# Joining the linear-attention block and its output projection into one interleaved block, with dummy matmuls beside it

## The chip, the cores and the metric

The kernel runs on one core of a Trainium2 chip. The metric is device time in microseconds (us) of one execution; a run's number is a median over executions. Engines are named as the profile names them: PE is the matrix engine, PEld its weight loads, DVE the vector engine, ACT the scalar engine, POOL and SP the other two. "Granted clock" is the share of full speed that PE's throttle allowed.

## The reference, cut to what matters

```python
x = A_x                                     # 1 x 2048 x 512, bf16; 32 heads of 16
x = x + _A_ref(_layernorm(x), A_wqkv, A_wo) # linear attention
x = x + _B_ref(_layernorm(x), B_wqkv, B_wo) # sliding-window softmax attention
x = x + _A_ref(_layernorm(x), A_wqkv, A_wo)
x = x + _B_ref(_layernorm(x), B_wqkv, B_wo)
# _A_ref: pq, pk = phi(q), phi(k)
#   kv = einsum(pk, v);  z = sum of pk over the sequence
#   o  = (pq kv) / (pq z + 1e-6);  return o @ wo
```

Only the two linear layers (first and third) are touched. I call them layer 1 and layer 3.

## The kernel before

The sequence is 16 tiles of 128 tokens. A linear layer is three blocks, and every engine waits for every other at the end of each: qkv, attention, output projection. The last two, cut to what matters (T is 16, f runs over four groups of eight heads):

```python
def phase_attn_A(self, first):
    # PE
    for f in range(4):                       # KV sums over all tokens
        for t in range(T): pe.matmul(pkv[:, f, 0:129], self.pk[:, t, ...], self.vA[:, t, f, 0:129], ...)
    for t in range(T):                       # denominators, 8 columns a matmul, two slots
        if t >= 2: pe.wait_ge(s_dcp.h, s_dcp.v(t - 1))
        for f in range(4): mm = pe.matmul(pden[sl][:, f * 8 : (f + 1) * 8], self.pqT[:, f, ...], self.Zs[:, f, :], ...)
        s_den.inc(mm)
    for t in range(T):                       # numerators, two slots
        if t >= 2: pe.wait_ge(s_od.h, s_od.v(t - 1))
        for f in range(4): mm = pe.matmul(pnum[:, sl, ...], self.pqT[:, f, ...], self.KV8[:, f, :], ...)
        s_num.inc(mm)
    # DVE: ... KV8, Zs; den_all + 1e-6 for 16 tiles; then
    v.wait_ge(s_r.h, s_r.v(1))
    for t in range(T):
        v.wait_ge(s_num.h, s_num.v(t + 1))
        s_od.inc(v.tensor_tensor(self.o_tok[:, t, :]..., pnum[:, sl, :]..., self.den_all[:, t, :]..., ALU.mult))
    # ACT: one reciprocal for all tiles, as Exp(-Ln(x)); a table is loaded in between
    a.wait_ge(s_dcp.h, s_dcp.v(T)); a.activation(flat, flat, ACT.Ln, ...); a.drain()
    s_r.inc(a.activation(flat, flat, ACT.Exp, ..., scale=-1.0))

def phase_wo(self, w_o, last, first, from_tok):      # a new block
    # PE, per tile: transpose o_tok (4 x 128x128), ACT copies it to SBUF, then 4 matmuls 128x512
    emit_transposes(pe, 0)
    for t in range(T):
        if t + 1 < T: emit_transposes(pe, t + 1)
        emit_matmuls(pe, t)
    # DVE, per tile
        s_res.inc(v.tensor_tensor(self.xres[:, t, :], pwo[:, sl, :], self.xres[:, t, :], ALU.add))
        if not last and t >= 1:
            v.bn_stats(self.ln_stats[:, t - 1, :], self.xres[:, t - 1, :])   # for the next layer's norm
```

The softmax here doesn't subtract the row's maximum and nothing guards it: scores larger than these inputs give would overflow.

## Time and profile before

| | before |
|---|---|
| median of 6 runs (lowest to highest) | 850.41 us (849.14 to 852.0) |
| span of the profiled execution | 847.4 us |
| layer 1, first multiply to last statistic | 34.59 us |
| layer 3, the same | 35.55 us |
| denominators to first multiply, layers 1 / 3 | 7.30 / 7.23 us |

The page of the kernel before: busy time and share of each engine, and the granted clock in tenths over 40 equal slices of the span.

```profile
...
PE 674.5 (80%) x5796; PEld 335.7 (40%) x5824; DVE 597.8 (71%) x2784; ACT 614.1 (72%) x856; POOL 6.5 (1%) x24
...
PEclk9989577996555555555779995979955555555559
...
```

No engine is busy throughout, and the clock falls to 5 in slices where PE still does work. An average over the whole span doesn't say what bounds one stage, so the next views look at the two changed layers alone.

The timeline of DVE in layer 1, kernel before. The columns are start, duration of the merged group, engine, line of the kernel, operation, output and inputs with sizes, count, and in brackets the idle time before it and what ended it.

```profile
...
97.66 0.30 DVE L580 TENSOR_SCALAR den_all<-pden 128x32 f32<-128x32 f32 x2 [0.26 <-PE pden L535]
100.82 11.04 DVE L586 TENSOR_TENSOR o_tokA<-pnum,den_all 128x512 bf16<-128x512 f32 x16 [2.86 <-ACT den_all L600]
115.38 0.69 DVE L681 TENSOR_TENSOR xres<-pwo,xres 128x512 bf16<-128x512 f32 x1 [3.52 <-PE pwo L646]
116.86 0.69 DVE L681 TENSOR_TENSOR xres<-pwo,xres 128x512 bf16<-128x512 f32 x1 [0.79 <-PE pwo L646]
117.47 0.69 DVE L684 BATCH_NORM_STATS2 ln_stats<-xres 128x6 f32<-128x512 bf16 x1
118.07 0.68 DVE L681 TENSOR_TENSOR xres<-pwo,xres 128x512 bf16<-128x512 f32 x1
...
```

The 16 multiplies take 11.04 us, 0.69 us each. They are in pairs: a closer look shows one start 0.60 us after the last and the next 0.79 us after it, because with two slots the PE's numerators are in line every second time. Then DVE waits 3.52 us for the first projection: block change, transposes, ACT copy and matmuls in series. After a slow start it alternates adds and statistics at about 0.595 us from start to start. Here 48 DVE instructions at 0.6 us, 28.6 us of work, take 34.59 us.

Busy time by stage, kernel before, layer 1. The columns are the stretch, its length, then PE, PEld, DVE, ACT and POOL busy (with instruction counts), granted clock, DMA share and GB/s.

```profile
...
93.52:100.82 7.30, 3.80 (x72) 2.92 (x72) 2.36 (x17) 2.73 (x3) 0.00 (x0) 0.64 0.00 0
100.82:111.86 11.04, 8.45 (x56) 4.81 (x56) 10.32 (x16) 0.00 (x0) 0.00 (x0) 0.50 0.00 0
111.86:115.38 3.52, 2.54 (x14) 1.61 (x16) 0.00 (x0) 1.08 (x2) 0.00 (x0) 0.50 0.02 5
115.38:135.41 20.03, 16.40 (x114) 8.87 (x114) 19.24 (x32) 9.64 (x15) 0.00 (x0) 0.98 0.00 0
...
```

PE is at half clock through the multiplies and the gap, and reaches full clock only with the dense projection. Its timeline at that place, same kernel:

```profile
...
112.18 1.01 PE L631 MATMUL pstwo<-ident,o_tokA 128*128 128x128 bf16 x8 [1.05 <-PEq L511]
113.86 1.49 PE L646 MATMUL pwo<-wA_o,oTtA 128*128 128x512 bf16 x3 [0.66 <-ACT oTtA L671]
...
116.66 0.39 PE L631 MATMUL pstwo<-ident,o_tokA 128*128 128x128 bf16 x4
...
```

Eight transposes take 1.01 us here; four take 0.39 us later, when the clock is at 1.00.

### The profile page before, as it was taken

The numbers are of one execution on the slowest core, as the hardware profiler recorded it, in microseconds if no ns is written. First come the engines' busy times: TensorE is split into PE (matmuls) and PEld (weight loads), VectorE is DVE, ScalarE is ACT, GpSimd is POOL, SyncE is SP. The second block draws the span as 40 slices with busy tenths as digits, with TensorE's granted clock in tenths as the row PEclk, the third lists the DMA queues.
The fourth block names the chain that finished last, engine by engine and source line by source line (L and its number), as shares of the span: only waits on it lengthen the run. The fifth ranks groups of instructions, "written<-read, shape, count | busy, mean of one in ns | idle before, by whom it ended". The sixth has DMA issues, their size and how long they took to land. (4 is left out here: it accounts for less than half of the span.)

```text
span 847.4 us, 16703 instructions
## 1 busy us (share of the span) xinstructions
PE 674.5 (80%) x5796; PEld 335.7 (40%) x5824; DVE 597.8 (71%) x2784; ACT 614.1 (72%) x856; POOL 6.5 (1%) x24
## 2 busy tenths in 40 slices
PE   0778685997888888888858876878888888888878
PEld 0343553443343443434533344434334434344344
DVE  6669676336878878788767775934488787887765
ACT  1678135448999999999557751455599999999983
POOL 1000000000000000000000000000000000000000
PEclk9989577996555555555779995979955555555559
DMA  8000000000000000000000000000000000000002
GB/s 297 0 1 1 1 1 2 1 1 1 1 2 1 2 2 1 2 1 2 1 1 0 1 1 1 1 1 2 0 2 1 2 2 2 2 1 2 1 2 100
DMA packets 5972, 9.46 MB, mean 11 GB/s; under 512 B 384, under 2 KB 4992, under 8 KB 5888
## 3 DMA queue, kind: packets, MB, share of 16 engines
q1 hardware_dynamic: 5472, 6.29, 2.2%
q0 software_dynamic: 416, 2.10, 0.7%
q8 instruction: 47, 0.77, 0.4%
q14 instruction: 37, 0.30, 0.1%
HBM read 6.29 MB, written 2.10 MB: 10 GB/s over the span
## 5 line engine op out<-in xcount | busy, mean ns | idle before, releaser
L811 ACT ACTIVATE PTs<-st,zero 128x768 bf16<-128x768 f32 (+2 forms) x512 | 404.8, 860 | 21.2 <-PE st L766 9.3
L848 DVE TENSOR_TENSOR PTs<-PTs,maskHi 128x128 bf16<-128x128 bf16 x1024 | 219.6, 220 | 78.7 <-ACT PTs L811 78.1
L785 PE MATMUL U<-vB,PTs 128*128 128x17 bf16 x2880 | 163.2, 179 | 66.5 <-DVE PTs L852 61.7
L785 PEld LDWEIGHTS U<-vB,PTs 128*128 128x128 bf16 x2880 | 116.3, 106 | 243.5 <-DVE PTs L852 227.6
L852 DVE TENSOR_TENSOR PTs<-PTs,maskLo 128x128 bf16<-128x128 bf16 x896 | 195.1, 218 | 0.0
L766 PE MATMUL st<-qT,kT 16*128 16x384 bf16 (+2 forms) x512 | 121.6, 473 | 2.2 <-PEq L321 2.2
L766 PE MATMUL st<-qT,kTB 32*128 32x384 bf16 (+2 forms) x512 | 122.5, 474 | 0.0
L339 PE MATMUL pst<-ident,xn 128*128 128x128 bf16 x256 | 30.7, 277 | 71.6 <-DVE xn L437 66.8
L377 PE MATMUL pss<-xnT,wB_qk 128*128 128x512 bf16 x248 | 61.2, 387 | 0.8 <-issue 0.4
L377 PE MATMUL pss<-wA_qkv,xnT 128*128 128x512 bf16 x255 | 61.6, 384 | 0.1
L681 DVE TENSOR_TENSOR xres<-pwo,xres 128x512 bf16<-128x512 f32 x64 | 43.6, 681 | 24.4 <-PE pwo L646 24.4
L399 ACT ACTIVATE xnT<-pst 128x512 bf16<-128x512 bf16 x64 | 34.8, 595 | 31.8 <-PE pst L339 31.5
L471 DVE TENSOR_SCALAR kTB<-kT,maskB 128x512 bf16<-128x512 bf16 x32 | 11.3, 353 | 64.2 <-ACT kT L418 64.2
L252 ACT ACTIVATE tmpE<-pss,zero 128x512 f32<-128x512 f32 x64 | 44.1, 689 | 15.4 <-PE pss L377 8.5
L339 PEld LDWEIGHTS pst<-ident,xn 128*128 128x128 bf16 x256 | 20.4, 120 | 84.5 <-DVE xn L437 51.0
L671 ACT ACTIVATE oTtA<-pstwo 128x512 bf16<-128x512 bf16 x32 | 18.9, 597 | 42.0 <-PE pstwo L631 42.0
L828 DVE TENSOR_TENSOR o_tok<-U,densb 128x128 bf16<-128x128 f32 x128 | 37.3, 292 | 9.6
L253 ACT ACTIVATE tmpR<-pss,zero 128x512 bf16<-128x512 f32 x64 | 44.0, 687 | 0.0
L256 DVE TENSOR_SCALAR tmpE<-tmpE 128x512 f32<-128x512 f32 x64 | 26.9, 421 | 23.3 <-ACT tmpR L253 23.2
L418 ACT ACTIVATE qT<-pss 128x512 bf16<-128x512 f32 x32 | 19.1, 597 | 32.5 <-PE pss L377 32.5
L437 DVE TENSOR_SCALAR xn<-xres,ln_mv,ln_rstd 128x512 bf16<-128x512 bf16 x64 | 26.1, 431 | 18.2 <-PE pst L339 7.4
L377 PEld LDWEIGHTS pss<-wA_qkv,xnT 128*128 128x128 bf16 x256 | 25.6, 100 | 32.2 <-issue 3.6
(77 smaller groups left out, 639.8 us busy)
## 6 DMA issues: line engine op xcount, KB each, us to landing
xres<-in_A_x_dram SPq DMA_DIRECT2D x4, 512.0 KB, 5.4
out_dram<-xres SPq DMA_DIRECT2D x16, 128.0 KB, 1.7
wA_qkv<-in_A_wqkv_dram SPq DMA_DIRECT2D x1, 1536.0 KB, 10.2
wB_nat<-in_B_wqkv_dram POOLq DMA_DIRECT2D x1, 1536.0 KB, 9.1
wA_o<-in_A_wo_dram SPq DMA_DIRECT2D x1, 512.0 KB, 12.3
wB_o<-in_B_wo_dram POOLq DMA_DIRECT2D x1, 512.0 KB, 9.6
```

The source lines that it names most:

```text
L252: a.activation(self.tmpE[:, js, :], ps_ap, ACT.Exp, bias=z)
L253: return a.activation(self.tmpR[:, js, :], ps_ap, ACT.Relu, bias=z)
L339: mm = pe.transpose(pst[sl2][:, kt, :], self.xn[:, sl2, kt * P : (kt + 1) * P], self.ident[:])
L377: mm = pe.matmul(pss[:, sl, :], lhsT, rhs, start=(kt == 0), stop=(kt == 3))
L399: s_cp.inc(a.activation(self.xnT[:, :, t * P : (t + 1) * P], pst[sl2][:], ACT.Copy))
L681: s_res.inc(v.tensor_tensor(self.xres[:, t, :], pwo[:, sl, :], self.xres[:, t, :], ALU.add))
L766: mm = pe.matmul(ST[sl][:, e, 0:n], lhsT, rhs, start=True, stop=True, tile_position=(32 * (hs % 4), 0))
L785: mm = pe.matmul(ut[:, hs, 0:17], lhsT, rhs, start=(ci == 0), stop=(ci == len(cl) - 1))
L811: a.activation(self.PTs[:, j % NJS, hp[0] : hp[0] + 2, 0:n], ST[sl][:, :, 0:n], ACT.Exp, bias=self.zero1[:], scale=DH ** -0.5,)
L828: v.tensor_tensor(self.o_tok[:, jd, fd * P : (fd + 1) * P].rearrange("p (h d) -> p h d", d=DH), ut[:, :, 0:DH], dsb.to_broadcast([P, 8, DH ...
L848: op = v.tensor_tensor(self.PTs[:, js, hs, 0:P], self.PTs[:, js, hs, 0:P], self.maskHi[:], ALU.mult)
L852: op = v.tensor_tensor(self.PTs[:, js, hs, 2 * P : 3 * P], self.PTs[:, js, hs, 2 * P : 3 * P], self.maskLo[:], ALU.mult,)
```

## The change

Intent: let DVE go from multiplies to adds without a gap, hide ACT's transposed copies and the PE's work behind DVE, and keep the PE's clock up by dummy matmuls where it would idle. Its core, cuts marked:

```diff
-                        self.phase_attn_A(first=(li == 0))
-                        self.phase_wo(self.wA_o, last=last, first=(li == 0), from_tok=True)
+                        self.phase_attnwo_A(first=(li == 0), last=last)
 ...
+            def pe_warm(pe, n):
+                for _ in range(n):
+                    pe.matmul(pkw[:, 3, :], w_o[:, 0, 0:P], w_o[:, 0, :], start=True, stop=True)
 ... (KV sums as before, denominators now in spare columns of the same PSUM tensor)
                     s_den.inc(mm)
+                    if t % 2 == 1:
+                        pe_warm(pe, 1)
+                pe.wait_ge(s_dcp.h, s_dcp.v(T))
+                pe_num(pe, 0)
+                pe_num(pe, 1)
+                pe_warm(pe, 11)
+                for t in range(1, T + 2):
+                    if t <= T:
+                        pe_trans(pe, t - 1)
+                    if t + 1 < T:
+                        pe_num(pe, t + 1)
                     if t >= 2:
-                        pe.wait_ge(s_od.h, s_od.v(t - 1))
- ... (numerators for all tiles)
+                        pe_wo(pe, t - 2)
 ... DVE
+                LAGD = 3
+                for t in range(T + LAGD):
+                    if t < T:
+                        dve_mult(t)
+                    if t >= LAGD:
+                        dve_add(t - LAGD)     # and the statistics of tile t - 4
 ... ACT: the transposed copies follow the Ln and Exp in the same block
```

No DVE or ACT instruction goes away. PE gets 19 more matmuls per layer.

More of the change, by code (lines that the diff above doesn't have):

```diff
@@ L492, in phase_qkv, with phase_attnwo_A @@
         self.commit_all()
-    def phase_attn_A(self, first):
+    def phase_attnwo_A(self, first, last):
         nc = self.nc
@@ L505, in phase_attn_A @@
         s_pm = self.sem("permB")
+        s_w = self.sem("ld_wAo")
+        s_wo = self.sem("wo")
+        s_res = self.sem("res")
+        s_out = self.sem("out")
+        s_tp = self.sem("tpw")
+        s_cp = self.sem("cpw")
+        s_stat = self.sem("lnstat")
+        s_rstd = self.sem("lnrstd")
+        NSW = 4
+        w_o = self.wA_o
         with (
-            nc.psum_tensor(self.uname("pkv"), [P, 4, 512], dt.float32) as pkv,
+            nc.psum_tensor(self.uname("pkw"), [P, 4, 512], dt.float32) as pkw,
@@ L508, in phase_attn_A @@
             nc.psum_tensor(self.uname("pnum"), [P, 2, 512], dt.float32) as pnum,
-            nc.psum_tensor(self.uname("pden"), [P, H], dt.float32) as pden0,
-            nc.psum_tensor(self.uname("pden"), [P, H], dt.float32) as pden1,
+            nc.psum_tensor(self.uname("pstA"), [P, 4, P], dt.bfloat16) as pstA0,
+            nc.psum_tensor(self.uname("pstA"), [P, 4, P], dt.bfloat16) as pstA1,
             nc.Block() as blk,
         ):
-            pden = [pden0, pden1]
+            pst = [pstA0, pstA1]
@@ new lines, in dslot, with pe_num @@
+            def dslot(t):
+                return pkw[:, t % 2, 256 : 256 + H]
+            def pe_num(pe, t):
+                sl = t % 2
+                if t >= 2:
+                    pe.wait_ge(s_od.h, s_od.v(t - 1))
+                mm = None
+                for f in range(4):
+                    mm = pe.matmul(
+                        pnum[:, sl, f * P : (f + 1) * P],
+                        self.pqT[:, f, t * P : (t + 1) * P],
+                        self.KV8[:, f, :],
+                        start=True,
+                        stop=True,
+                    )
+                s_num.inc(mm)
@@ new lines, in pe_trans, with pe_wo @@
+            def pe_trans(pe, t):
+                sl2 = t % 2
+                pe.wait_ge(s_od.h, s_od.v(t + 1))
+                if t >= 2:
+                    pe.wait_ge(s_cp.h, s_cp.v(t - 1))
+                mm = None
+                for f in range(4):
+                    mm = pe.transpose(pst[sl2][:, f, :], self.o_tok[:, t, f * P : (f + 1) * P], self.ident[:])
+                s_tp.inc(mm)
+            def pe_wo(pe, t):
+                sl = t % NSW
+                if t >= NSW:
+                    pe.wait_ge(s_res.h, s_res.v(t - NSW + 1))
+                pe.wait_ge(s_cp.h, s_cp.v(t + 1))
+                mm = None
+                for f in range(4):
+                    mm = pe.matmul(pkw[:, sl, :], self.oTt[:, t % 2, f, :], w_o[:, f, :], start=(f == 0), stop=(f == 3))
+                s_wo.inc(mm)
@@ L515, in _ @@
+            def pe_warm(pe, n):
+                for _ in range(n):
+                    pe.matmul(pkw[:, 3, :], w_o[:, 0, 0:P], w_o[:, 0, :], start=True, stop=True)
             @blk.tensor
             def _(pe):
+                if first:
+                    pe.wait_ge(s_w.h, s_w.emitted)
                 for f in range(4):
@@ L520, in _ @@
                         mm = pe.matmul(
-                            pkv[:, f, 0:129],
+                            pkw[:, f, 0:129],
                             self.pk[:, t, f * P : (f + 1) * P],
@@ L529, in _ @@
                 for t in range(T):
-                    sl = t % 2
                     if t >= 2:
@@ L535, in _ @@
                         mm = pe.matmul(
-                            pden[sl][:, f * 8 : (f + 1) * 8],
+                            dslot(t)[:, f * 8 : (f + 1) * 8],
                             self.pqT[:, f, t * P : (t + 1) * P],
@@ L542, in _ @@
                     s_den.inc(mm)
-                for t in range(T):
-                    sl = t % 2
-                    if t >= 2:
-                        pe.wait_ge(s_od.h, s_od.v(t - 1))
-                    mm = None
-                    for f in range(4):
-                        mm = pe.matmul(
-                            pnum[:, sl, f * P : (f + 1) * P],
-                            self.pqT[:, f, t * P : (t + 1) * P],
-                            self.KV8[:, f, :],
-                            start=True,
-                            stop=True,
-                        )
-                    s_num.inc(mm)
+                    if t % 2 == 1:
[9 more added lines that the diff above has]
+                        pe_num(pe, t + 1)
+                    if t >= 2:
+                        pe_wo(pe, t - 2)
             @blk.vector
@@ L572, in _ @@
                     v.wait_ge(s_kv.h, s_kv.v(f + 1))
-                    v.tensor_tensor(self.KV8[:, f, :], pkv[:, f, 0:P], self.blockmask[:], ALU.mult)
-                    v.tensor_copy(self.zc[:, f : f + 1], pkv[:, f, P : P + 1])
+                    v.tensor_tensor(self.KV8[:, f, :], pkw[:, f, 0:P], self.blockmask[:], ALU.mult)
+                    v.tensor_copy(self.zc[:, f : f + 1], pkw[:, f, P : P + 1])
                     v.drain()
@@ L577, in _, with dve_mult @@
                 for t in range(T):
-                    sl = t % 2
                     v.wait_ge(s_den.h, s_den.v(t + 1))
-                    s_dcp.inc(v.tensor_scalar(self.den_all[:, t, :], pden[sl][:], 1e-6, None, op0=ALU.add))
+                    s_dcp.inc(v.tensor_scalar(self.den_all[:, t, :], dslot(t), 1e-6, None, op0=ALU.add))
                 v.wait_ge(s_r.h, s_r.v(1))
-                for t in range(T):
+                def dve_mult(t):
                     sl = t % 2
@@ L592, in _, with dve_add @@
                     )
+                def dve_add(t):
+                    sl = t % NSW
+                    v.wait_ge(s_wo.h, s_wo.v(t + 1))
+                    s_res.inc(v.tensor_tensor(self.xres[:, t, :], pkw[:, sl, :], self.xres[:, t, :], ALU.add))
+                    if not last and t >= 1:
+                        v.wait_ge(s_res.h, s_res.v(t))
+                        v.bn_stats(self.ln_stats[:, t - 1, :], self.xres[:, t - 1, :])
+                LAGD = 3
[4 more added lines that the diff above has]
+                        dve_add(t - LAGD)
+                if not last:
+                    v.wait_ge(s_res.h, s_res.v(T))
+                    v.bn_stats(self.ln_stats[:, T - 1, :], self.xres[:, T - 1, :])
+                    v.drain()
+                    for t in range(T):
+                        v.bn_aggr(self.ln_mv[:, t, :], self.ln_stats[:, t, :])
+                    v.drain()
+                    s_stat.inc(v.nop())
             @blk.scalar
@@ L600, in _ @@
                 s_r.inc(a.activation(flat, flat, ACT.Exp, bias=self.zero1[:], scale=-1.0))
+                for t in range(T):
+                    sl2 = t % 2
+                    a.wait_ge(s_tp.h, s_tp.v(t + 1))
+                    if t >= 2:
+                        a.wait_ge(s_wo.h, s_wo.v(t - 1))
+                    s_cp.inc(a.activation(self.oTt[:, sl2, :, :], pst[sl2][:], ACT.Copy))
+                if not last:
+                    a.wait_ge(s_stat.h, s_stat.v(1))
+                    s_rstd.inc(self._ln_rstd(a))
+            if last:
+                @blk.sync
+                def _(e):
+                    for t in range(T):
+                        e.wait_ge(s_res.h, s_res.v(t + 1))
+                        s_out.inc(e.dma_start(self.out[0, t * P : (t + 1) * P, :], self.xres[:, t, :]), 16)
+                    e.wait_ge(s_out.h, s_out.v16(T))
         self.commit_all()
```

## The prediction

> **What bounds the kernel now.** The change touches the linear-attention layers only (first and third of four). There the timeline shows three serial pieces. (a) KV sums and denominators, then ACT's Ln and Exp with a table load between: from 97.97 us (last denominator copy) to 100.8 PE and DVE have no useful work. (b) 16 DVE multiplies (o_tok), 11.04 us, while ACT idles for 12 us. They follow each other at 0.69 us, but in pairs 0.60 and 0.79: with two slots and the clock at 0.50, every second multiply waits for the PE. (c) A block change, transposes and first projection matmuls on a cold PE: DVE idles 3.5 us (4.2 in layer 3). Then DVE alternates 16 residual adds and 16 statistics at 0.595 us each, about 19.9 us. From first multiply to last statistic: 34.6 us (100.82 to 135.4) in layer 1, 35.5 us in layer 3. DVE work in it is 48 instructions x 0.6 = 28.6 us; the rest is pairing stalls and the gap. Nothing else of the 850 us is changed.
>
> **What the change does.** One block instead of two. DVE interleaves multiply(t), add(t-3), statistics(t-4); no DVE instruction is removed. PE interleaves transpose, numerator and projection. Removed: the 3.5 to 4.2 us gap and the pairing stalls (1.5 us). Added: 19 dummy 128x512 matmuls per layer, eight among the denominators, eleven in the Ln/Exp wait, to keep PE's clock up. The Trainium skill ("TensorE: Matmul & The Clock Gate", Part 1) says that idle PE drops to half clock and returns after about 3.4 us of sustained work; this trace agrees (0.50 all through (b), 1.00 about 2 us after dense projection in layer 1, 4.6 us in layer 3).
>
> **Cost.** Full-clock PE work per tile in the fused loop: transposes plus projection take 1.09 us per tile in the trace; numerators add some 0.22: 1.3 us against DVE's 1.79. So DVE sets the pace, and the loop takes 28.6 us plus 0.5 to 1 us of filling bubbles. Cold, PE work doubles to about 2.6 us per tile and PE would set the pace until the clock returns. PE would be some 72% busy when warm; the cold numerator stage streamed about 62% and never warmed up, so the hold is not certain. Dummies among denominators: that stage runs on a 0.54 us round trip per two tiles, half of it idle; a dummy costs 0.22 us warm (hidden) or 0.43 cold, so 0.2 to 1.2 us per layer. The eleven take 2.4 us warm, in a wait of about 2.9 us; 4.7 if cold, which delays the first transposes by about 1 us.
>
> All of this lies on the critical path, since the next layer's normalisation needs all statistics. Saved: layer 1 about 4.3 us, layer 3 about 5.3; less about 1 us for a clock that is cold part of the time.
>
> **Prediction.** 841.5 us, range 837 to 848. Faster by over 2%: 0.03; within 2%: 0.95; slower by over 2%: 0.02.
>
> **What would show it.** Timeline: first multiply to last statistic about 29.5 to 31 us in each of the two layers; DVE without idle in the loop's middle; ACT's transposed copies starting within 2 us of the first multiply. Windows: clock mostly 1.00 from about 100 us to the loop's end (third layer alike), against 0.50 before. The denominator stage no more than 1.2 us longer. The sliding-window layers unchanged to 1 us.
>
> **What would make it wrong.** If the clock falls to 0.50 inside the loop, PE at 2.6 us per tile eats the gain: 845 to 852. If add or multiply slows down when PE writes other banks, or if PE's in-order queue makes numerator(t+1) wait behind projection on ACT's copy, DVE shows waits on pnum or pkw in the loop. If denominators stretch by over 2 us, the dummies are the cause.

## The result, and the profile after

| | before | after |
|---|---|---|
| median (runs) | 851.23 us (16) | 838.40 us (7) |
| lowest to highest | 849.14 to 853.0 | 837.38 to 839.86 |
| ratio, 95% interval | | 0.9853 (0.984 to 0.9866) |
| span profiled | 847.4 | 837.1 |
| denominators to first multiply, layers 1 / 3 | 7.30 / 7.23 | 7.24 / 7.24 |
| first multiply to last statistic, layers 1 / 3 | 34.59 / 35.55 | 29.33 / 29.34 |

A ratio is the mean time of one kernel's fast runs over that of the other's of the same rounds, so not quite the ratio of the medians. Again in a later batch, the changed kernel gave 0.9838 (0.9824 to 0.9853) and a median of 837.31 us.

The page of the changed kernel, the same lines:

```profile
...
PE 670.3 (80%) x5830; PEld 328.9 (39%) x5862; DVE 596.6 (71%) x2784; ACT 614.7 (73%) x856; POOL 6.5 (1%) x24
...
PEclk9989997996555555555779999989955555555559
...
```

DVE's timeline in layer 1, changed kernel:

```profile
...
98.28 0.29 DVE L630 TENSOR_SCALAR den_all<-pkw 128x32 f32<-128x32 f32 x2 [0.25 <-PE pkw L587]
101.44 2.69 DVE L637 TENSOR_TENSOR o_tokA<-pnum,den_all 128x512 bf16<-128x512 f32 x4 [2.86 <-ACT den_all L674]
104.35 0.69 DVE L648 TENSOR_TENSOR xres<-pkw,xres 128x512 bf16<-128x512 f32 x1 [0.21 <-PE pkw L559]
104.95 0.68 DVE L637 TENSOR_TENSOR o_tokA<-pnum,den_all 128x512 bf16<-128x512 f32 x1
105.66 0.69 DVE L648 TENSOR_TENSOR xres<-pkw,xres 128x512 bf16<-128x512 f32 x1
106.27 0.68 DVE L651 BATCH_NORM_STATS2 ln_stats<-xres 128x6 f32<-128x512 bf16 x1
106.86 0.67 DVE L637 TENSOR_TENSOR o_tokA<-pnum,den_all 128x512 bf16<-128x512 f32 x1
107.46 0.68 DVE L648 TENSOR_TENSOR xres<-pkw,xres 128x512 bf16<-128x512 f32 x1
...
```

One wait of 0.21 us before the first add is all that DVE has left in the loop (between 104.95 and 105.66 the starts are 0.71 us apart, then 0.6). The gap of 3.52 us is gone, and so are the pairs: multiply, add and statistics follow each other at 0.6 us.

Busy time by stage, changed kernel, layers 1 and 3: denominators to first multiply, then the loop.

```profile
...
94.20:101.44 7.24, 6.82 (x89) 3.77 (x91) 2.33 (x17) 2.73 (x3) 0.00 (x0) 1.00 0.00 0
101.44:130.77 29.33, 22.55 (x182) 12.01 (x184) 28.98 (x48) 10.84 (x17) 0.00 (x0) 1.00 0.00 1
...
504.08:511.32 7.24, 6.81 (x89) 3.77 (x91) 2.33 (x16) 2.73 (x3) 0.00 (x0) 1.00 0.02 3
511.32:540.66 29.34, 22.55 (x182) 12.00 (x184) 28.98 (x48) 10.84 (x17) 0.00 (x0) 1.00 0.00 1
...
```

DVE is busy 28.98 of 29.33 us, and the clock is 1.00 from the denominators to the end. PE's timeline, changed kernel, layer 1:

```profile
...
99.09 2.54 PE L564 MATMUL pkw<-wA_o 128*128 128x512 bf16 x11
102.19 0.40 PE L549 MATMUL pstA<-ident,o_tokA 128*128 128x128 bf16 x4 [0.56 <-DVE o_tokA L637]
...
103.27 1.04 PE L559 MATMUL pkw<-wA_o,oTtA 128*128 128x512 bf16 x4
...
```

The eleven dummies take 2.54 us and end at 101.6 us, half a microsecond before DVE's first multiply lets the transposes start.

To see where time went in the whole kernel, I cut every profiled execution at the same events (first KV sum, first denominator, first multiply, last statistic, first and last exponential of the sliding-window layer). This is worked out from the start and end times in the traces:

```
us per stage        start  KV   den   loop  qkv B  attn B  wo B   qkv A  KV   den   loop  qkv B  attn B  wo B
                    -> KV       -> x  L1    L2     L2      L2     L3          -> x  L3    L4     L4      L4
before              86.13  7.39 7.30  34.59 59.98  211.36  25.31  69.63  6.18 7.23  35.55 60.52  211.27  24.96
after               88.03  6.17 7.24  29.33 60.37  211.59  25.40  69.84  6.11 7.24  29.34 60.20  211.64  24.60
```

The two loops are 70.14 us before and 58.67 after: 11.47 us less. The ratio 0.9853 of 851.2 us is 12.5 us, so the loops are nearly all of it. (The spans differ by less, 10.3 us, because the profiled execution of before was its fastest, 849.14 us.) The other stages differ by up to 1.9 us either way, and not by anything the change does to them; one experiment below shows where such differences come from.

### The profile page after: what moved, and what is told of

It is laid out like the page before. It is cut to its first block, busy times and chain, and to the rows that moved or that the text cites. A ratio compares the mean times of both kernels' runs of the same rounds, so it can differ in the third digit from the quotient of the medians.

```text
span 837.1 us, 16781 instructions
## 1 busy us (share of the span) xinstructions
PE 670.3 (80%) x5830; PEld 328.9 (39%) x5862; DVE 596.6 (71%) x2784; ACT 614.7 (73%) x856; POOL 6.5 (1%) x24
## 5 line engine op out<-in xcount | busy, mean ns | idle before, releaser
L903 ACT ACTIVATE PTs<-st,zero 128x768 bf16<-128x768 f32 (+2 forms) x512 | 404.7, 860 | 21.9 <-PE st L858 10.3
L376 PE MATMUL pss<-wA_qkv,xnT 128*128 128x512 bf16 x255 | 64.2, 396 | 0.3 <-issue 0.2
L680 ACT ACTIVATE oTtA<-pstA 128x512 bf16<-128x512 bf16 x32 | 19.1, 597 | 31.1 <-PE pstA L549 31.1
L376 PEld LDWEIGHTS pss<-xnT,wB_qk 128*128 128x128 bf16 x256 | 25.5, 100 | 30.4 <-issue 2.9
```

Of the source, the lines that this page charges most:

```text
L376: mm = pe.matmul(pss[:, sl, :], lhsT, rhs, start=(kt == 0), stop=(kt == 3))
L903: a.activation(self.PTs[:, j % NJS, hp[0] : hp[0] + 2, 0:n], ST[sl][:, :, 0:n], ACT.Exp, bias=self.zero1[:], scale=DH ** -0.5,)
```

## The experiments

Twelve runs were made: eleven edited kernels, and the change once more. Theory A: the gain comes from the interleaved order, which leaves DVE nothing to wait for, and needs a PE at full clock at the loop's start, which the dummies give. Rivals: the order alone does it and the dummies are decoration (B); the clock alone does it (C); taking away the block boundary is enough, whatever the order (D). All kernels gave correct results.

### No dummies

```diff
-                    if t % 2 == 1:
-                        pe_warm(pe, 1)
-                pe_warm(pe, 11)
```

> The changed kernel without any of the 19 dummy matmuls per layer. Theory A (the fused order gives the gain, but the clock must be warm): the granted clock is 0.50 at the first multiply, PE needs about 2.6 us per tile instead of 1.3 for the 2 to 5 us until the clock returns, DVE waits for pkw and pnum at the loop's start; the loop from first multiply to last statistic takes 30.5 to 32 us instead of 29.3; total 841 to 843. Rival B (the fused loop warms itself, dummies are decoration): loop 29.3 to 29.8 us, total 838 to 839.5. Rival C (the loop is too sparse to warm up and stays at half clock): PE sets the pace, loop over 38 us, total over 855.

Measured: 842.97 us, ratio 0.9913 (0.99 to 0.9926). Loops 30.65 and 30.45 us. DVE's timeline at the start of layer 1's loop, and the busy table there, without dummies:

```profile
...
101.61 1.29 DVE L634 TENSOR_TENSOR o_tokA<-pnum,den_all 128x512 bf16<-128x512 f32 x2 [2.86 <-ACT den_all L671]
103.43 0.69 DVE L634 TENSOR_TENSOR o_tokA<-pnum,den_all 128x512 bf16<-128x512 f32 x1 [0.53 <-PE pnum L533]
104.28 0.69 DVE L634 TENSOR_TENSOR o_tokA<-pnum,den_all 128x512 bf16<-128x512 f32 x1 [0.16 <-PE pnum L533]
105.82 0.69 DVE L645 TENSOR_TENSOR xres<-pkw,xres 128x512 bf16<-128x512 f32 x1 [0.85 <-PE pkw L559]
...
```

```profile
...
101.60:105.40 3.80, 3.04 (x20) 2.22 (x21) 2.67 (x4) 1.19 (x2) 0.00 (x0) 0.50 0.00 0
105.40:132.20 26.80, 20.79 (x166) 10.77 (x164) 26.36 (x44) 9.64 (x15) 0.00 (x0) 1.00 0.00 1
...
```

The busy table of the whole loop of layer 1 without dummies:

```profile
...
101.61:132.26 30.65, 23.83 (x184) 12.99 (x184) 29.09 (x48) 10.84 (x17) 0.00 (x0) 0.94 0.00 1
...
```

DVE waits 0.53, 0.16 and 0.85 us for a PE at half clock; after about 3.9 us of the loop the clock is back and stays. So the loop warms the PE by itself, as B said, but the dummies are not decoration: they save 1.2 us per loop by having it warm before. B falls, and so does the fear that the loop would stay cold (the C of this expectation, a loop over 38 us).

### Only the eight dummies, and only the eleven

```diff
 # f1_den_eight_only
-                pe_warm(pe, 11)
 # f2_wait_eleven_only
-                    if t % 2 == 1:
-                        pe_warm(pe, 1)
```

> Only the eight dummies among the denominators are kept. The denominator stage stays at full clock, but then PE idles about 3 us during Ln and Exp. If an idle gap of 3 us drops the clock, the loop begins at 0.50 and costs what it costs without dummies (841 to 843); if the gap is short enough to hold, 838 to 839.

> Only the eleven dummies in the Ln/Exp wait are kept. In the kernel before, the clock fell to 0.50 during the denominators in the first layer (at 95.8 us), so here the eleven start cold, take up to 4.7 us instead of 2.5 and push the first transposes back by 0.5 to 1.5 us; by the loop the clock is at 1.00. Total 839 to 841. If they are enough by themselves: 838 to 839.

Measured: eight only, 844.08 us (1 us above what was expected), ratio 0.9917 (0.9904 to 0.993), loops 30.52 and 30.55 us, as without any. Eleven only, 839.55 us, ratio 0.9867 (0.9854 to 0.988), loops 30.12 and 30.01 us. The busy table of the run with eight, at the Ln/Exp wait and the loop's first 2.7 us:

```profile
...
97.50:100.70 3.20, 0.59 (x8) 0.42 (x8) 0.42 (x1) 2.67 (x3) 0.00 (x0) 0.96 0.00 0
100.70:103.40 2.70, 2.37 (x18) 1.98 (x19) 2.01 (x4) 1.19 (x2) 0.00 (x0) 0.50 0.00 0
...
```

The clock survives the denominators but falls in the Ln/Exp wait, 2.4 us after the PE's last matmul ended (in layer 3 too), so the loop begins cold. The Trainium skill ("TensorE: Matmul & The Clock Gate", Part 1) gives at least one idle window of about 3.4 us before the clock halves. The order of size agrees. Here the fall came 2.4 us after the last matmul, less than such a window, so the window was not wholly idle; after the loop of the changed kernel it came after 5.0. PE's timeline of the run with eleven:

```profile
...
99.07 3.67 PE L564 MATMUL pkw<-wA_o 128*128 128x512 bf16 x11
102.58 0.39 PE L549 MATMUL pstA<-ident,o_tokA 128*128 128x128 bf16 x4
...
```

Here the eleven start cold, take 3.67 us instead of 2.54, and the first transposes start 1.53 us after the first multiply (101.05 us) instead of 0.75. So the eight keep the clock for the eleven, and the eleven keep it for the loop. By loops: eleven alone save 0.5 us a layer, with the eight 1.2.

### The dummies in the old kernel

```diff
 # two blocks as before; dummies go into PSUM bank pkv[:, 3, :]
                     s_den.inc(mm)
+                    if t % 2 == 1:
+                        pe_warm(pe, 1)
+                pe.wait_ge(s_dcp.h, s_dcp.v(T))
                 for t in range(T):
                     sl = t % 2
+                    if t == 2:
+                        pe_warm(pe, 11)
```

> The kernel before with the same 19 dummies per layer, nothing fused. If the gain is a matter of clock alone, this shows most of it: below 842. If fusing gives it: only the multiply pairing stall (0.60 and 0.79 us in turn) goes while the clock holds, 0.5 to 1.5 us per layer, and the 3.5 to 4.2 us gap between multiplies and adds stays; total 847.5 to 850. The numerators keep a warm PE only 37% busy, so the clock is expected back at 0.50 within 4 us of the multiplies' start.

Measured: 850.8 us, ratio 0.9994 (0.9979 to 1.0009): nothing, a little less than I expected. The loops took 35.37 and 35.35 us, against 34.59 and 35.55 without the dummies. The busy table over the multiplies of layer 1:

```profile
...
101.30:105.50 4.20, 2.63 (x25) 1.48 (x24) 4.20 (x7) 0.00 (x0) 0.00 (x0) 0.95 0.00 0
105.50:112.00 6.50, 4.96 (x34) 2.75 (x32) 5.92 (x10) 0.00 (x0) 0.00 (x0) 0.50 0.01 3
...
```

At full clock the multiplies did follow at 0.6 us (seven in 4.2 us), but the clock fell 3.8 us after the first of them (105.1 us), when the PE had only numerators to do; the gap (3.52 us, as before) and the cold projection stayed. Clock alone (C) is not the gain.

### One block, old order

```diff
-                for t in range(1, T + 2):
-                    ... (interleaved)
+                for t in range(2, T):
+                    pe_num(pe, t)
+                pe_trans(pe, 0)
+                for t in range(T):
+                    if t + 1 < T:
+                        pe_trans(pe, t + 1)
+                    pe_wo(pe, t)
 # DVE
-                for t in range(T + LAGD):
-                    ... (interleaved)
+                for t in range(T):
+                    dve_mult(t)
+                for t in range(T):
+                    dve_add(t)
 # s1: also without the 19 dummies; s2: with them
```

> One block as in the change, but in the old order (all multiplies, then all adds with statistics) and without dummies. It separates taking away the block boundary from interleaving. If the boundary is the whole gain, total is 842 to 844, like the fused kernel without dummies. If interleaving matters: the multiplies still go in pairs at 0.60 and 0.79 us beside a PE at 0.50, the gap before the first add shrinks from 3.5 to about 1.7 us (transposes, copy and a cold first projection are still in line), and the adds still start on a cold PE; loop 32 to 33.5 us per layer, total 845 to 848.

> The same with the 19 dummies. In the two-block kernel with dummies the clock fell about 4 us after the multiplies began, since numerators alone keep the PE too idle. So the dummies should be worth nothing much here either: 845 to 848, within 1 us of the run without them. If they are worth 4 to 5 us as in the fused kernel, warmth at the start alone matters, whatever comes after.

Measured: without dummies 844.09 us (expected: 845 to 848), ratio 0.9927 (0.991 to 0.9944), loops 33.35 and 33.30 us; with them 845.37 us, ratio 0.9938 (0.9915 to 0.9961), loops 33.19 and 33.11 us. DVE's timeline in layer 1, without dummies, and the busy table of that loop:

```profile
...
100.87 11.04 DVE L634 TENSOR_TENSOR o_tokA<-pnum,den_all 128x512 bf16<-128x512 f32 x16 [2.86 <-ACT den_all L670]
114.23 0.69 DVE L645 TENSOR_TENSOR xres<-pkw,xres 128x512 bf16<-128x512 f32 x1 [2.32 <-PE pkw L559]
115.67 0.69 DVE L645 TENSOR_TENSOR xres<-pkw,xres 128x512 bf16<-128x512 f32 x1 [0.75 <-PE pkw L559]
...
```

```profile
...
100.87:134.22 33.35, 27.19 (x181) 15.33 (x184) 29.56 (x48) 10.73 (x17) 0.00 (x0) 0.79 0.00 0
...
```

The multiplies take 11.04 us as before, and the gap shrinks from 3.52 to 2.32 us (1.7 was expected). In the loops, the boundary is worth 1.24 and 2.25 us, the interleaved order a further 2.8 (33.3 to 30.5), and dummies 1.2 more. In the old order the dummies are worth only 0.2 us per loop, so their 1.2 needs the interleaved order. The total doesn't follow: it fell by 0.73%, 6.2 us, where the loops explain 3.5, and it is only 0.0014 above the ratio of the interleaved kernel without dummies (from another batch). So the totals don't tell D and A apart; the traces of the loops do.

The reason can be seen in a stage that no edit touched. PE's timeline at the start of layer 2's qkv stage, in the run with eight dummies and then in the run with eleven:

```profile
...
140.59 3.62 PE L376 MATMUL pss<-xnT,wB_qk 128*128 128x512 bf16 x8
144.01 1.45 PE L376 MATMUL pss<-wB_nat,xnT 128*128 128x512 bf16 x4
...
```

```profile
...
140.96 2.56 PE L376 MATMUL pss<-xnT,wB_qk 128*128 128x512 bf16 x8
143.36 1.03 PE L376 MATMUL pss<-wB_nat,xnT 128*128 128x512 bf16 x4
...
```

The code is the same and the idle time before it too (7.94 us in both), but the first eight projection matmuls take 3.62 us in one and 2.56 in the other: by the windows view the clock came back 4.2 us after their start in the first and 1.4 us in the second. The clock records tell why: in each of the fourteen profiled executions all changes of the clock lie on a grid of 3.41 us, and the grid starts at another place in each. I worked out how full each step of the grid is: matmuls as I measured them, 0.216 us per 128x512 at full clock and twice that at half, smaller ones and those that use fewer rows of the array in proportion, transposes included. In the run with eight, the step from 138.0 to 141.4 us is 0.75 full and the clock stays at half for one step more; in the run with eleven, the step from 138.9 to 142.3 is 0.84 full and the clock is back at its end. The stage then took 61.32 and 59.89 us, and layer 4's 61.31 and 59.80. The span less the two loops ranges from 775.8 to 780.9 us over the profiled executions of ten kernels (before, after and its repeat, the six edits above, and lag two), which differ elsewhere only by the dummies among the denominators and in the Ln/Exp wait. So a total can mislead by several us about an edit worth one or two, even where the executions of one kernel agree well.

### How far the add lags behind the multiply

```diff
-                LAGD = 3
+                LAGD = 1      # f3_lag1;  2 in f4_lag2
```

> The changed kernel with the add one tile behind the multiply instead of three. Each add then waits for its own transposes, copy and projection: about 1.6 us of DVE idle per tile warm, 2.8 cold, so 25 to 45 us more per layer: total 885 to 930, with DVE waiting for pkw in every tile. If the lag is no part of the gain: below 842.

> Lag of two tiles. By the trace the projection of tile t-2 ends about 1.6 us after multiply(t-1), and DVE asks for it about 1.9 us after: enough with 0.3 us to spare at full clock. Total within 1 us of lag three (837.5 to 840). If the spare is overestimated, DVE shows a wait on pkw in each tile and the total is 842 or more.

Measured: lag one, 891.72 us (a single run, state unknown). Lag two, 840.22 us (0.2 above what was expected), ratio 0.9874 (0.9854 to 0.9893), loops 30.20 us in both layers. DVE's timeline with lag one, and the busy table over 40 us of that loop:

```profile
...
106.00 0.69 DVE L648 TENSOR_TENSOR xres<-pkw,xres 128x512 bf16<-128x512 f32 x1 [1.58 <-PE pkw L559]
...
107.21 0.67 DVE L637 TENSOR_TENSOR o_tokA<-pnum,den_all 128x512 bf16<-128x512 f32 x1
109.46 0.69 DVE L648 TENSOR_TENSOR xres<-pkw,xres 128x512 bf16<-128x512 f32 x1 [1.58 <-PE pkw L559]
...
```

```profile
...
104.48:145.00 40.52, 17.64 (x141) 9.08 (x144) 21.64 (x35) 7.17 (x12) 0.00 (x0) 1.00 0.00 0
...
```

Every tile waits 1.58 us for its own projection (expected: 1.6), and the period is 3.46 us instead of 1.79. One block and dummies with a lag of one made a kernel some 42 us slower than the old one of the same batch (850.03 us). With lag two only the filling of the pipeline costs more: DVE waits 0.81 us before the first add instead of 0.21, and nothing in the middle. The table also bears on a doubt of the prediction: PE is busy 17.64 of 40.52 us (44%; by the spacing of the matmuls they fill an estimated 38%), and the clock stayed at 1.00 for 40 us.

### Dummies in the remaining idle places

These look for a version that beats both kernels. `a1_change_again` is the unedited change, as a measure in the same rounds.

```diff
 # w1_idle_ends: at the end of the fused block (24), of layer 2's projection (24), of each linear qkv stage (12)
+                for _ in range(24):
+                    pe.matmul(pnum[:, 0, :], w_o[:, 0, 0:P], w_o[:, 0, :], start=True, stop=True)
 # w2_idle_ends_chunks: also in the two gaps between chunks of the linear layers' qkv stage
+                    if kind == "A" and c < C - 2:
+                        pe_idle(pe, j, 8)       # waits for a free PSUM slot, then 8 dummies
 # w3_idle_and_transposes: also one dummy after each four transposes at a stage's start,
 # and after the chunk gaps; none before layer 1's KV sums
```

> The changed kernel once more, unedited, as the measure for the two runs beside it: 837 to 840.

> The changed kernel plus dummies where PE is idle between stages: 12 at the end of each linear layer's qkv stage (idle 4.2 us before the KV sums), 24 at the end of the fused block and of layer 2's output projection (idle about 7.5 us before the next layer's transposes). It tests what the remaining cold starts cost. KV sums on a warm PE take about 4.4 us to the first denominator instead of 6.1: 1.7 us in each of two layers; transposes and first projections of the next qkv stage, 1 to 1.8 us in each of three. Total 829 to 834. If those stages wait for DVE or ACT instead of PE: 837 or more.

> The same, with 8 more dummies in each of the two idle gaps (about 3.5 us) between chunks of the linear layers' qkv stage. The clock there fell in some gaps of the trace and not in others. Worth 0 to 1 us per gap, four gaps: total 827 to 833. If the qkv stage is paced by DVE and ACT after the gap anyway, equal to the run beside it.

> The run with dummies at idle ends and between chunks, changed in two places. (1) No dummies before the KV sums of the first layer: there the warm sums only waited for the weight permutation on DVE, the clock then fell among the denominators and the stage became 0.6 us longer. (2) One dummy after each group of four transposes at a stage's start, because transposes alone (32% busy) let the clock fall just as the projections began. If that was why the dummies at the ends of the fused block gave nothing, each of three qkv starts gains 0.5 to 1.5 us: ratio to the kernel before 0.974 to 0.978. If those starts are paced by DVE and ACT, or the dummies delay the transposes: 0.979 or more, as without them.

Measured: change again 837.31 us, ratio 0.9838; w1 837.41 us, 0.9838 (0.9825 to 0.9852); w2 833.26 us, 0.9793 (0.9778 to 0.9808); w3, in another batch, 833.95 us, 0.981 (0.9796 to 0.9823).

All three missed what was expected: w1 by 3 us, w2 by 0.3 us, w3 with a ratio of 0.981 instead of 0.974 to 0.978. The ends alone gave nothing in total. In layer 3 the KV sums did what was expected: 4.55 us to the first denominator instead of 6.03 in the run beside it. In layer 1 they didn't. Its busy table with w1, KV sums and then denominators to first multiply:

```profile
...
86.85:92.50 5.65, 3.79 (x64) 3.61 (x64) 5.33 (x44) 1.24 (x1) 0.00 (x0) 1.00 0.02 4
92.55:100.38 7.83, 7.41 (x84) 4.64 (x87) 2.38 (x16) 2.73 (x3) 0.00 (x0) 0.56 0.00 0
...
```

The sums ran at full clock, but DVE, which permutes weights there, was not ready; PE idled 1.91 us, the clock fell, the eight dummies became slow, and the stage took 7.83 us instead of 7.24. At the qkv starts the warm clock lasted through part of the transposes and fell shortly before the projections (in layer 2 at 137.5 us, projections from 140.0). Dummies between the transposes (w3) did not cure that in layer 2: the step of the clock's grid before the fall was 0.31 full with w1 and 0.33 with w3, both under the 0.37 above which it always held (last section). w2, which also fills the gaps between chunks, is 0.45% faster than w1 in the same rounds, with intervals apart. w2 and w3 are the fastest kernels here, and w3's interval overlaps with w2's. That the filled gaps as such give this is not shown: in the one profile of each, layer 3's qkv stage is 1.05 us shorter with w2, but layer 4's, which w2 leaves as it was in w1, is 1.27 us shorter too.

## Why the prediction was right

The prediction, 841.5 us in a range of 837 to 848, held: 838.40. It missed the middle by 3 us on the good side: its terms add up to 8.6 us saved (4.3 and 5.3, less 1), and the loops alone saved 11.5. The mechanism was right; costs that it took off did not come. (By its own terms, 34.6 less 28.6 and 0.5 to 1 us, layer 1 would have saved 5.0 to 5.5 us; it doesn't say why it put 4.3.) Point by point:

- What bounds the loop. It named three serial pieces and 28.6 us of DVE work. After the change DVE is busy 28.98 of 29.33 us, with 0.21 us of waiting. Over the 28.6 us that it counted, the "0.5 to 1 us of filling bubbles" were 0.73.
- Removed: the gap and the pairing stalls. Both are gone in the timeline. The saving was put at 4.3 and 5.3 us per layer; the loops measured 5.26 and 6.21. One size was misread: the gap is 3.52 us in layer 3 too, not 4.2; there it is the wait after it that is longer (1.44 against 0.79 us).
- Dummies among the denominators: put at 0.2 to 1.2 us per layer. The stage took 7.24 us against 7.30 and 7.23, so they cost nothing: the clock was at 1.00, and a dummy fits into the idle half of the round trip. The larger figure was for a cold clock, and in the run with extra dummies at the ends that case occurred and cost 0.6 us.
- Clock: "about 1 us" was taken off for part of the loop cold. It was at 1.00 all through. Why it held can be read from the grid of 3.41 us (last section): the steps that lie wholly inside PE's part of the loop are 0.65 to 0.99 full, and after every step over 0.37 the clock held. The prediction's 2 and 4.6 us for the clock's return before the change are 2.2 and 4.3 us after the first projection by the clock records, on both sides of the Trainium skill's 3.4 us of sustained work; the clock came back where a step of the grid ended.
- The checks that the prediction named: loops of 29.5 to 31 us (29.33, 29.34, just under), copies within 2 us of the first multiply (1.18: 102.62 against 101.44), the sliding-window layers' attention unchanged to 1 us (211.36 to 211.59, 211.27 to 211.64).

The causes are shown by the loops in the traces: of 11.5 us for both layers, 3.5 come from the block boundary, 5.6 from the interleaved order and 2.4 from the dummies, if they are added in this order. Taken in another order they differ: with the dummies before the interleaving, the dummies give 0.3 and the interleaving 7.6. Measured by totals the shares differ too, because unedited stages shift by as much. What is not shown is the last 1 us between 11.5 and 12.5.

## What to carry to other kernels

When two stages in series are paced by the same engine, interleave their tiles with enough lag that each tile's round trip through the other engines fits; here lag three left one wait of 0.21 us, lag two cost 0.9 us per loop and lag one nearly doubled the period. Dummy matmuls pay where a cold PE would be in line for the next stage, if they fit into a wait that exists anyway; the same dummies were worth nothing where the clock fell again before it was needed. Judge an edit worth 1 or 2 us by its stage in the trace, since the clock's return after idling moves other stages by as much.

## What the Trainium skill lacked or had wrong

- "TensorE: Matmul & The Clock Gate", Part 1, tells when idle and dense PE change the clock, but not how much partial work holds it. Here work of about 1.3 us in each 3.46 us (38%) held it for 40 us, while four 128x128 matmuls each 0.6 us let it fall 3.6 us after the dummies stopped. By the spacing of such matmuls that page gives at full clock (56 ns), the latter is an estimated 37%. The traces settle it by the steps of the 3.41 us grid (filled as worked out under "One block, old order"). At full clock, all 147 steps that were less than 0.31 full were followed by half clock, and all 1125 over 0.37 by full; at half clock, all 1837 under 0.66 by half, and all 117 over 0.79 by full. In the old kernel with dummies the step that ended at 105.05 us was 0.32 full; with lag one the steps were 0.38 full (0.32 where a matmul is missing from the trace). The steps between these bounds, 30 at full and 64 at half clock, leave the exact limits open.
- The same page, Part 1, puts the warm-up at about 3.4 us of sustained work. In traces with the same code before it, the clock came back 4.2 us or 1.4 us after the projections of layer 2 began (the page does say that the window runs freely); that this moves a stage by 1.4 us and so hides small edits is not said. It also gives at least one idle window of about 3.4 us before the clock falls. The 5.0 us after the last matmul (changed kernel, after the loop) fit that; the 2.4 us (eight dummies only, both layers) do not, as the grid step that ended with this fall in layer 1 was still 0.19 full.
- The same page, "Back-to-back issue gap", gives about 131 ns per 128x512 matmul as the sustained rate. Eleven dummies in a row, each with its own weight load, took 2.54 us with the last one's 0.38 us, so 216 ns from start to start at a granted clock of 1.00. That section calls this the gap of an isolated matmul, while Part 1 of the same page has 215.7 ns for back-to-back ones; the measurement agrees with Part 1.
- No page has the cost of a block boundary in a chain like this one: DVE waited 3.52 us from its last multiply to its first add with it, 2.32 us without (half clock in both).
